# Splitting float64 weights by shifts of the high word, with the low word's share on GpSimd

## Chip, cores and metric

One NeuronCore of a Trainium2 chip runs the whole program in one launch. The metric is the device time of one execution in microseconds, lower is better. Engines are called TensorE (PE, and PEld for its weight loads), VectorE (DVE), ScalarE (ACT), GpSimd (POOL) and SyncE (SP, which issues most of the transfers).

## The reference

Three parts follow each other: an mLSTM attention over 4 x 8 heads of 768 tokens, a mixture of 8 experts with one expert for each token, and a gated MLP over all 3072 tokens of width 320:

```python
def _moe_ref(x, expert_emb, tau, w1, w2):        # N, D, E, F = 3072, 320, 8, 1024
    ...
    for e in range(E):
        mask = expert_idx == e
        h = np.maximum(x[mask] @ w1[e], 0.0)
        out[mask] = gate_w[mask, None] * (h @ w2[e])

def _moe2_ref(x, w_in, w_out):                   # d_ff = 2048
    h = x @ w_in
    g = h * (1.0 / (1.0 + np.exp(-1.702 * h)))
    return (g @ w_out).astype(np.float32)
```

`w_in` (320 x 2048) and `w_out` (2048 x 320) reach the kernel as float64, all other inputs as float32.

## The kernel before

The kernel multiplies in float32 by two parts: a value is split into a high part of type float32r and the rest, and a product is the sum of high times high, high times rest and rest times high. Each weight is therefore split once before it is used.

The expert stage has 64 steps, s = e * 8 + m: expert e (the first four with 512 tokens, the last four with 384) and block m of 128 hidden columns. A step issues, in this order: `h_mm` (8 matmuls into `hp`), `relu_split` (ScalarE writes the high part `hh`, VectorE the rest `hl`, L1094), `tail` of the step before (`o_mm`, three matmuls for each 128 tokens, which need `hh` and `hl`), `split_w` of the expert weights of six steps later (ScalarE casts at L105 and L118, GpSimd subtracts 256 columns at L110, VectorE 64x128 at L111 and 128x320 at L121), `prep_x` in some steps (TensorE transposes the next expert's tokens, ScalarE writes `xh`, VectorE `xl`, L1056), every second step one indirect transfer `meta_put` on GpSimd's queue, and from s = 6 on `convert`.

`convert` prepares the MLP's weights while the expert stage runs. There are 16 blocks m: 384 columns of w_in and 320 of w_out, float64, loaded as pairs of 32-bit words into tile `c` (two buffers). `cvt` turns a pair into a float32 value `fr`: ScalarE scales the low word (L1156), VectorE takes exponent, sign and mantissa out of the high word with four `TENSOR_SCALAR` operations (`ex`, `sb`, `mt`) and joins them with three two-input operations (L1163, L1165, L1167). It is a generator in five parts, of which a call of `convert(n)` runs n: 4 or 3 a step for the experts with 512 tokens and 2 for those with 384, and 3 in each of the 16 steps of block E, the MLP's first. After the last part, `then` splits `fr` one call later like any weight: `split_w1` into `win` (ScalarE cast, GpSimd subtraction L110, VectorE L111), `split_w2` into `wout` (ScalarE L118, VectorE L121). `fr` has two buffers, `ex`, `sb` and `mt` one.

After the expert stage the MLP runs over blocks of tokens, E first: `h_mm` from `win`, `swish_split` (ScalarE sigmoid, VectorE product, ScalarE cast, VectorE `hhl`, L1104 to L1107), `o_mm` from `wout`. `scale_y` multiplies the next block's tokens on GpSimd (L1244).

The whole is issued in a manual schedule: each engine works through its instructions in the order in which the program issues them.

Of the kernel before, what the change touches and what calls it, by code (L numbers as in the profile page):

```python
# [1 line left out]

# [7 lines left out]
F32 = mybir.dt.float32  # L10
F32R = mybir.dt.float32r
BF16 = mybir.dt.bfloat16
I32 = mybir.dt.int32
AF = mybir.ActivationFunctionType
ALU = mybir.AluOpType
# [4 lines left out]
P = 128  # L20
CAP = 512
# [5 lines left out]
def kernel(ctx, tc, qT_in, kT_in, kvo_in, i_gate, f_gate, expert_emb, tau, w12, wio, out, dbg=None):  # L27
# [71 lines left out]
    def split_w1(t, r1):  # L99

        split_w1hi(t, r1)
        split_w1lo(t, r1)
# [10 lines left out]
    def split_w2(t, r2):  # L113
        split_w2hi(t, r2)
        split_w2lo(t, r2, nc.vector)
# [890 lines left out]
    with ExitStack() as mctx:  # L1006
# [137 lines left out]
                tc.add_to_no_dep_group("out", sc.ins)  # L1144


        U32 = mybir.dt.uint32

        def cvt(src, n, then):

            lo, hi = src[:, :, 0], src[:, :, 1]
            ex = mp2.tile([P, n], I32, tag="ex", name="ex", bufs=1)
            sb = mp2.tile([P, n], I32, tag="sb", name="sb", bufs=1)
            mt = mp2.tile([P, n], I32, tag="mt", name="mt", bufs=1)
            fr = mp2.tile([P, n], F32, tag="fr", name="fr")
            nc.scalar.activation(out=fr, in_=lo.bitcast(U32), func=AF.Copy, scale=2.0 ** -52)  # L1156
            nc.vector.tensor_scalar(out=ex, in0=hi, scalar1=20, scalar2=0x7ff, op0=ALU.logical_shift_right, op1=ALU.bitwise_and)  # L1157
            nc.vector.tensor_scalar(out=sb, in0=hi, scalar1=-2147483648, scalar2=None, op0=ALU.bitwise_and)  # L1158
            yield
            nc.vector.tensor_scalar(out=mt, in0=hi, scalar1=0xfffff, scalar2=None, op0=ALU.bitwise_and)  # L1160
            nc.vector.tensor_scalar(out=ex, in0=ex, scalar1=896.0, scalar2=0.0, op0=ALU.subtract, op1=ALU.max)
            yield
            nc.vector.scalar_tensor_tensor(out=fr, in0=mt, scalar=2.0 ** -20, in1=fr, op0=ALU.mult, op1=ALU.add)  # L1163
            yield
            nc.vector.scalar_tensor_tensor(out=ex, in0=ex, scalar=float(2 ** 23), in1=sb, op0=ALU.mult, op1=ALU.add)  # L1165
            yield
            nc.vector.scalar_tensor_tensor(out=fr, in0=fr, scalar=1.0, in1=ex.bitcast(F32), op0=ALU.add, op1=ALU.mult)  # L1167
            late.append(lambda: then(fr))
            yield

        craw, late = {}, []

# [5 lines left out]
        def cvt_all():  # L1178
            for m in range(M2):
                if 0 < m < M2 - 1:  # L1180
                    load_c(m + 1)
                t = craw.pop(m)
                yield from cvt(t[:, 0:3 * P], 3 * P, lambda r, m=m: split_w1(win[:, m], r.rearrange("p (c f) -> p c f", c=3)))
                yield from cvt(t[:, 3 * P:], DM, lambda r, m=m: split_w2(wout[:, m], r))

        tokd = mp1.tile([P, NTILE], I32, name="tokd")
        gated = mp1.tile([P, NTILE], F32, name="gated")
# [189 lines left out]
        with tc.manual_schedule():  # L1377
            load_x0(1)
            flag = nc.values_load(vals_i[0:1, 2 * E:2 * E + 1], min_val=0, max_val=1)
            with tc.If(flag > 0):  # L1380
                general()
            touch()
            load_x0(0)
            for p in range(1, E):
                ids[p] = nc.values_load(vals_i[0:1, p:p + 1], engines=sp, min_val=0, max_val=E - 1)
                if p == 1:
                    load_w(WA // 2 + 1)
                    for c in range(3):
                        prep_x0(1, c)
                    load_x(1)  # L1390
                    load_w(WA // 2 + 2)
            offs = {p: nc.values_load(vals_i[0:1, E + p:E + p + 1], engines=sp, min_val=0, max_val=NT) for p in range(1, E)}

            steps = [(e, m, e * M1 + m) for e in range(E) for m in range(M1)]
            prev = None
            conv = cvt_all()

            def convert(n):

                now, late[:] = late[:], []  # L1400
                for f in now:
                    f()
                for _ in range(n):
                    next(conv, None)

            def tail(p):
                e, m, s = p
                o_mm(e, ("a", s), wslot.pop(s)[1], m == 0, m == M1 - 1)
                if m == M1 - 1:
                    put(e)  # L1410

            for e, m, s in steps:
                h_mm(e, ("a", s), wslot[s][0], EARLY if s in he else 0)
                relu_split(("a", s))
                if s in he:
                    hs_t["a", s] = halves(*he.pop(s)) + hs_t["a", s]
                if prev:
                    tail(prev)
                prev = (e, m, s)
                if 1 <= s < 4:  # L1420
                    prep_x0(0, s - 1)
                if s == 1:
                    gts = gates_1()
                if s == 2:
                    gates_2(*gts)
                if s == 3:
                    order_rows()
                if s == 4:
                    meta_tile()

                for w in [] if s == 0 else [s + WA - 1] if s < WA else [s + WA - 1, s + WA] if s == WA else [s + WA]:
                    if w < NS1:
                        split_w(w)
                        if w % 2 and w // 2 + 3 < NS1 // 2:
                            load_w(w // 2 + 3)
                if e + 1 < E and 2 <= m - (e == 0) < 5:
                    prep_x(e + 1, m - 2 - (e == 0))
                if m == 5 + (e == 0) and e + 2 < E:
                    load_x(e + 2)
                if s % 2 == 0 and 0 <= s // 2 - 3 < NTILE:  # L1440
                    meta_put(s // 2 - 3)
                if s == 7 + 2 * NTILE:
                    meta_get()
                if s == 9 + 2 * NTILE:
                    meta_split()
                if e == E - 1:

                    if m == 1:
                        load_y(E)
                    if m == 3:  # L1450
                        scale_y(E, nc.vector)
                    if 4 <= m < 7:
                        prep_x(E, m - 4)
                    if m == 7:
                        load_y(E + 1)
                if s in (3, 5):
                    load_c((s - 3) // 2)
                if s >= WA:
                    convert(2 if CAPS[e] < CAP else 3 if 2 <= m < 6 else 4)

            def tail2(p):
                blk, m = p
                o_mm(blk, ("b", blk, m), wout[:, m], m == 0, m == M2 - 1)
                if m == M2 - 1:
                    put_out(blk)

            left = [prev]
            for blk in range(E, len(COLS)):
                for m in range(M2):
                    h_mm(blk, ("b", blk, m), win[:, m])  # L1470
                    swish_split(("b", blk, m))
                    left.append((blk, m))
                    while len(left) > (1 if ncol(blk) == CAP else 2):
                        p = left.pop(0)
                        (tail2 if len(p) == 2 else tail)(p)
                    if blk == E:
                        convert(3)
                    nxt = blk + 1
                    if nxt < len(COLS):
                        t = m - (2 if blk == E else 0)  # L1480
                        small = ncol(blk) < CAP
                        if t == 2:
                            scale_y(nxt, nc.vector if small else nc.gpsimd)
                        for j in range(ncol(nxt) // GH):
                            t0 = t - 3 * j
                            if 3 <= t0 < 5:
                                planes(nxt, j, t0 - 3)
                            w0 = t0 - (8 if small else 6)
                            if 0 <= w0 < 2:
                                words(nxt, j, w0)  # L1490
                            if 2 <= w0 < 5:
                                parts(nxt, j, w0 - 2)
                        if t == 8 and nxt + 1 < len(COLS):
                            load_y(nxt + 1)
            for p in left:
                tail2(p)
            if dbg is not None:
                nc.sync.dma_start(out=dbg["slot"], in_=slot_i)
                nc.sync.dma_start(out=dbg["lg"], in_=logit_all.rearrange("p t e -> p (t e)"))
                nc.sync.dma_start(out=dbg["ss"], in_=ss_all)  # L1500
# [62 lines left out]
```

## Time and profile before

| | us |
|---|---|
| median of 3 runs | 809.84 |
| lowest and highest of them | 806.26, 811.72 |
| profiled execution, its time | 813.04 |
| profiled execution, span of the trace | 811.3 |

In the profile a group of instructions is named by engine, line, operation and the tiles that it writes and reads (`out<-in`, shapes as partitions x elements). Its time is given as busy time and as the mean of one instruction; an idle time behind it is what the engine waited for just before, and what ended that. The timeline gives for each instruction its start, its duration, and in brackets the wait before it. TensorE's clock is given as a share of 2.4 GHz; its lower level is 1.2 GHz.

### The profile page before, as it was taken

Reading aid. Unit: us, or ns where it says so; the run is one execution under the profiler, and the core shown is the slowest. Engines: PE = TensorE matmul, PEld = TensorE weight load, DVE = VectorE, ACT = ScalarE, POOL = GpSimd, SP = SyncE. Lnnn points to the kernel's source line nnn. Section 1 sums busy time; section 2 is a strip of 40 time slices with the busy share of each in tenths; the row PEclk is TensorE's granted clock in tenths of the full one; section 3 lists DMA queues with packets and bytes.
Section 4 is the critical chain, followed back from the end, with each engine's and each line's share of the span. In section 5 each row is a group of like instructions: output and inputs, shape, how many; then the busy total and the mean of one; then the engine's idle time right before and its main releaser. Section 6 shows DMA issues by size and latency. Waiting matters only on the chain.

```text
span 811.3 us, 13142 instructions
## 1 busy us (share of the span) xinstructions
PE 749.3 (92%) x4708; PEld 695.9 (86%) x4708; DVE 577.4 (71%) x1209; ACT 340.8 (42%) x802; POOL 246.8 (30%) x362
## 2 busy tenths in 40 slices
PE   6789888998798999989998899999999999999995
PEld 6789888888797787888888789899899898999995
DVE  7887979988499999999997645555554554445542
ACT  4343332434464455555554334333343334334442
POOL 4553456686134334444531100300300300201011
PEclk9798978989899999999999999999999999999998
DMA  6977757662465645567743212021120110200100
GB/s 194 313 260 215 270 191 248 209 236 85 154 224 161 219 148 198 179 182 216 206 111 99 64 21 59 33 41 37 43 69 1 53 40 1 71 1 20 35 17 16
DMA packets 70302, 100.19 MB, mean 123 GB/s; under 512 B 31120, under 2 KB 56472, under 8 KB 70232
## 3 DMA queue, kind: packets, MB, share of 16 engines
q1 hardware_dynamic: 67160, 91.41, 37.0%
q0 software_dynamic: 3072, 7.89, 2.8%
q8 instruction: 38, 0.62, 0.3%
q14 instruction: 32, 0.26, 0.1%
HBM read 77.53 MB, written 17.82 MB: 118 GB/s over the span
## 4 chain that ended last, share of the span: by engine, by line
issue 41%; DVE 17%; PE 6%; POOL 5%; ACT 1%; POOLq 0%; DVEq 0%; ACTq 0%
DVE w L121 3%; POOL out_dram L1140 3%; DVE hl L1094 3%; PE hp L138 3%; DVE w L111 2%; DVE fr L1167 2%; POOL xr L1244 2%; DVE ex L1165 1%; PE acc L1119 1%; DVE fr L1163 1%; DVE ex L1157 1%; DVE mt L1160 1%; DVE xl L1056 1%; DVE sb L1158 1%; PE acc L1118 1%
## 5 line engine op out<-in xcount | busy, mean ns | idle before, releaser
L1105 DVE TENSOR_TENSOR sg<-hp,sg 128x512 f32<-128x512 f32 (+1 forms) x112 | 68.8, 615 | 100.7 <-ACT sg L1104 100.6
L138 PE MATMUL hp<-xh,win 128*128 128x512 f32 (+1 forms) x560 | 130.7, 363 | 0.0
L1107 DVE TENSOR_TENSOR hhl<-sg,hhl 128x512 fp32r<-128x512 f32 (+1 forms) x112 | 71.6, 639 | 70.0 <-ACT hhl L1106 70.0
L1117 PE MATMUL acc<-wout,hhl 128*128 128x320 f32 x384 | 118.4, 308 | 2.4 <-ACT hhl L1106 2.4
L1119 PE MATMUL acc<-wout,hhl 128*128 128x320 f32 x384 | 118.9, 310 | 0.2 <-DVE hhl L1107 0.2
L1118 PE MATMUL acc<-wout,hhl 128*128 128x320 f32 x384 | 118.7, 309 | 0.0
L1140 POOL DMA_INDIRECT out_dram<-o,tokd x24 | 23.7, 989 | 312.0 <-ACT o L1127 308.4
L1104 ACT ACTIVATE sg<-hp 128x512 f32<-128x512 f32 (+1 forms) x112 | 60.4, 539 | 133.0 <-PE hp L138 132.8
L138 PEld LDWEIGHTS hp<-xh,win 128*128 128x128 f32 x560 | 94.6, 189 | 10.5
L1106 ACT CAST hhl<-sg 128x512 fp32r<-128x512 f32 (+1 forms) x112 | 62.6, 559 | 81.2 <-DVE sg L1105 81.2
L138 PE MATMUL hp<-xl,win 128*128 128x512 f32 (+1 forms) x336 | 86.1, 365 | 0.0
L110 POOL TENSOR_TENSOR w<-r,w 128x256 fp32r<-128x256 f32 x58 | 48.2, 832 | 122.1 <-ACT w L105 119.7
L1119 PE MATMUL acc<-w,hl 128*128 128x320 f32 x212 | 68.9, 325 | 15.8 <-DVE hl L1094 15.4
L1117 PEld LDWEIGHTS acc<-wout,hhl 128*128 128x128 f32 x384 | 72.1, 188 | 6.2 <-ACT hhl L1106 2.8
L138 PE MATMUL hp<-xh,w 128*128 128x384 f32 (+2 forms) x320 | 75.9, 368 | 0.0
L1118 PEld LDWEIGHTS acc<-wout,hhl 128*128 128x128 f32 x384 | 72.2, 188 | 3.4
L1119 PEld LDWEIGHTS acc<-wout,hhl 128*128 128x128 f32 x384 | 72.2, 188 | 0.5 <-DVE hhl L1107 0.4
L138 PEld LDWEIGHTS hp<-xl,win 128*128 128x128 f32 x336 | 59.3, 190 | 11.2 <-DVE xl L1284 0.2
L1117 PE MATMUL acc<-w,hh 128*128 128x320 f32 x212 | 65.5, 309 | 0.0
L1118 PE MATMUL acc<-w,hh 128*128 128x320 f32 x212 | 65.4, 309 | 0.0
L360 DVE TENSOR_TENSOR_SCAN pm<-fb,ident_h 128x1024 f32<-128x1024 f32 x23 | 56.3, 2447 | 6.9 <-DMA fb<-dec 5.5
L400 PE MATMUL sp<-qT,kblk 120*128 120x128 f32 x384 | 57.8, 313 | 3.4 <-DVE wm L405 3.4
(315 smaller groups left out, 1526.4 us busy)
## 6 DMA issues: line engine op xcount, KB each, us to landing
r<-in_w_dram SPq DMA_DIRECT2D x32, 704.0 KB
fb<-dec SPq DMA_DIRECT2D x23, 512.0 KB
kvo<-in_kvo_dram SPq DMA_DIRECT2D x24, 480.0 KB
c<-in_wio_dram SPq DMA_DIRECT2D x16, 704.0 KB
rows<-zt SPq DMA_DIRECT2D x8, 640.0 KB
qT<-in_qT_dram SPq DMA_DIRECT2D x24, 180.0 KB
xr<-y SPq DMA_DIRECT2D x5, 640.0 KB
kblk<-in_kT_dram SPq DMA_DIRECT2D x48, 60.0 KB
```

The lines of the kernel that those rows point to most:

```text
L110: eng.tensor_tensor(out=t[:, 3 * P:5 * P].rearrange("p (c f) -> p c f", c=2), in0=r1[:, 0:2], in1=hif[:, 0:2], op=ALU.subtract)
L138: nc.tensor.matmul(hp, a, b, start=(i == 0), stop=(i == len(seq) - 1))
L360: nc.vector.tensor_tensor_scan(out=pm[u].rearrange("p h t -> p (h t)"), data0=fb[u].rearrange("p h t -> p (h t)"), data1=ident_h.rearrange ...
L400: nc.tensor.matmul(sp[:, h - hs.start], kblk[u % NLD][0:KR, h // 3, h % 3, :], qT[u][0:KR, h // 3, :], start=True, stop=True)
L1104: nc.scalar.activation(out=sg, in_=hp, func=AF.Sigmoid, scale=1.702)
L1105: nc.vector.tensor_tensor(out=g, in0=hp, in1=sg, op=ALU.mult)
L1106: nc.scalar.copy(hh, g)
L1107: nc.vector.tensor_tensor(out=hl, in0=g, in1=hh.bitcast(F32), op=ALU.subtract)
L1117: nc.tensor.matmul(a, hh, w[:, 0:DM], start=first, stop=False)
L1118: nc.tensor.matmul(a, hh, w[:, DM:2 * DM], start=False, stop=False)
L1119: nc.tensor.matmul(a, hl, w[:, 0:DM], start=False, stop=last)
L1140: sc = nc.gpsimd.indirect_dma_start(out=out, out_offset=bass.IndirectOffsetOnAxis(ap=tokd[:, ti:ti + 1], axis=0), in_=o[:, i], in_offset=None)
```

## The change

`cvt` is rewritten. The value's upper 32 bits come from the high word w1 by shifts and masks. ScalarE takes w1's absolute value as a float32 pattern (Abs), GpSimd limits it by a max and a min (`LEAST`, `MOST`), VectorE shifts it left by 3 with a mask and joins the sign bits (`shifts`), and takes from the result the power of two `pw`. In the next call (`rests`) ScalarE writes the high part `hi` straight into `win` or `wout`, GpSimd multiplies the scaled low word by `pw`, and GpSimd subtracts `hi` from the value. In the call after that (`sums`) VectorE adds the two rests into `lo`; for w_in with a second operation on 64 partitions.

So a matrix takes a start and three further calls of `convert`. A call first runs what is due of earlier matrices, then adds `thirds` to a counter and starts one matrix for each full three: 2 thirds a step for experts with 512 tokens, 1 for those with 384, 1 in each step of block E. `fr` and the new tile `rest` have two buffers, `pw` one. `split_w1` and `split_w2` are no longer called for these weights.

```diff
-        def cvt(src, n, then):
-            lo, hi = src[:, :, 0], src[:, :, 1]
...
-            nc.scalar.activation(out=fr, in_=lo.bitcast(U32), func=AF.Copy, scale=2.0 ** -52)
-            nc.vector.tensor_scalar(out=ex, in0=hi, scalar1=20, scalar2=0x7ff, op0=ALU.logical_shift_right, op1=ALU.bitwise_and)
-            nc.vector.tensor_scalar(out=sb, in0=hi, scalar1=-2147483648, scalar2=None, op0=ALU.bitwise_and)
-            yield
-            nc.vector.tensor_scalar(out=mt, in0=hi, scalar1=0xfffff, scalar2=None, op0=ALU.bitwise_and)
-            nc.vector.tensor_scalar(out=ex, in0=ex, scalar1=896.0, scalar2=0.0, op0=ALU.subtract, op1=ALU.max)
-            yield
-            nc.vector.scalar_tensor_tensor(out=fr, in0=mt, scalar=2.0 ** -20, in1=fr, op0=ALU.mult, op1=ALU.add)
-            yield
-            nc.vector.scalar_tensor_tensor(out=ex, in0=ex, scalar=float(2 ** 23), in1=sb, op0=ALU.mult, op1=ALU.add)
-            yield
-            nc.vector.scalar_tensor_tensor(out=fr, in0=fr, scalar=1.0, in1=ex.bitcast(F32), op0=ALU.add, op1=ALU.mult)
-            late.append(lambda: then(fr))
-            yield
+        LEAST, MOST = (struct.unpack("<f", struct.pack("<I", w))[0] for w in (0x38100000, 0x47EFFFFF))
+        def cvt(src, n, hi, lo):
+            w0, w1 = src[:, :, 0], src[:, :, 1]
+            pw = mp2.tile([P, n], I32, tag="pw", name="pw", bufs=1)
+            fr = mp2.tile([P, n], I32, tag="fr", name="fr")
+            rest = mp2.tile([P, n], F32, tag="rest", name="rest")
+            top, nl = fr.bitcast(F32), lo.shape[-1]
+            nc.scalar.activation(out=rest, in_=w0.bitcast(U32), func=AF.Copy, scale=2.0 ** -52)
+            nc.scalar.activation(out=top, in_=w1.bitcast(F32), func=AF.Abs)
+            nc.gpsimd.tensor_scalar(out=top, in0=top, scalar1=LEAST, scalar2=MOST, op0=ALU.max, op1=ALU.min)
+            def shifts():
+                nc.vector.tensor_scalar(out=fr, in0=fr, scalar1=3, scalar2=0x3ffffff8, op0=ALU.logical_shift_left, op1=ALU.bitwise_and)
+                nc.vector.scalar_tensor_tensor(out=fr, in0=w1, scalar=-0x40000000, in1=fr, op0=ALU.bitwise_and, op1=ALU.bitwise_or)
+                nc.vector.tensor_scalar(out=pw, in0=fr, scalar1=-0x800000, scalar2=None, op0=ALU.bitwise_and)
+            def rests():
+                nc.scalar.copy(hi, top)
+                nc.gpsimd.tensor_tensor(out=rest, in0=rest, in1=pw.bitcast(F32), op=ALU.mult)
+                nc.gpsimd.tensor_tensor(out=top, in0=top, in1=hi.bitcast(F32), op=ALU.subtract)
+            def sums():
+                nc.vector.tensor_tensor(out=lo, in0=top[:, 0:nl], in1=rest[:, 0:nl], op=ALU.add)
+                if nl < n:
+                    nc.vector.tensor_tensor(out=hi[64:P, nl:n], in0=top[64:P, nl:n], in1=rest[64:P, nl:n], op=ALU.add)
+            late.extend([(1, shifts), (2, rests), (3, sums)])
...
-                yield from cvt(t[:, 0:3 * P], 3 * P, lambda r, m=m: split_w1(win[:, m], r.rearrange("p (c f) -> p c f", c=3)))
-                yield from cvt(t[:, 3 * P:], DM, lambda r, m=m: split_w2(wout[:, m], r))
+                cvt(t[:, 0:3 * P], 3 * P, win[:, m, 0:3 * P], win[:, m, 3 * P:5 * P])
+                yield
+                cvt(t[:, 3 * P:], DM, wout[:, m, 0:DM], wout[:, m, DM:2 * DM])
+                yield
...
-            def convert(n):
-                now, late[:] = late[:], []
+            due = [0]
+            def convert(thirds):
+                now, late[:] = [f for k, f in late if k == 1], [(k - 1, f) for k, f in late if k > 1]
                 for f in now:
                     f()
-                for _ in range(n):
+                due[0] += thirds
+                while due[0] >= 3:
+                    due[0] -= 3
                     next(conv, None)
...
-                    convert(2 if CAPS[e] < CAP else 3 if 2 <= m < 6 else 4)
+                    convert(1 if CAPS[e] < CAP else 2)
...
-                        convert(3)
+                        convert(1)
```

## Rows read from the trace of the kernel before

**Rows 1.** The page, busy time of each engine over the span, with its share and its instructions.

```profile
PE 749.3 (92%) x4708; PEld 695.9 (86%) x4708; DVE 577.4 (71%) x1209; ACT 340.8 (42%) x802; POOL 246.8 (30%) x362
```

**Rows 2.** Busy time by stretch: the stretch in us from the span's start, its length, the busy time and instructions of PE, PEld, DVE, ACT and POOL, then the granted clock, the share of the DMA engines and GB/s. The stretches are the experts with 512 tokens from step 8 on, those with 384 up to step 63, and the beginning of block E.

```profile
240.56:347.20 106.64, 97.29 (x526) 84.74 (x525) 103.81 (x225) 53.89 (x122) 41.53 (x57) 0.98 0.56 178
347.20:447.18 99.98, 91.88 (x560) 87.53 (x559) 93.72 (x206) 54.27 (x130) 37.28 (x54) 1.00 0.60 165
447.18:470.00 22.82, 20.27 (x103) 17.59 (x102) 13.95 (x23) 8.95 (x16) 3.50 (x2) 0.93 0.17 55
```

**Rows 3.** Waits from 240.56 to 347.2 us: who waited for whom, us in total, times, the longest.

```profile
PE acc L1119 <- DVE hl L1094: 9.2, 12, 1.9
...
ACT fr L1156 <- DVE win L111: 7.4, 3, 3.7
...
ACT fr L1156 <- DVE wout L121: 5.0, 2, 2.6
```

**Rows 4.** Groups by line from 240.56 to 447.18 us, VectorE's and then GpSimd's tensor operations: count, busy us, mean ns of one, idle time before them.

```profile
L121 DVE TENSOR_TENSOR w<-r,w 128x320 fp32r<-128x320 f32 x51 | 30.4, 595 | 1.5
L111 DVE TENSOR_TENSOR w<-r,w 64x128 fp32r<-64x128 f32 x51 | 20.1, 395 | 1.6
L1167 DVE SCALAR_TENSOR_TENSOR fr<-fr,ex 128x384 f32<-128x384 f32 (+1 forms) x30 | 17.6, 586 | 0.7
...
L1157 DVE TENSOR_SCALAR ex<-c 128x320 int32<-128x320 int32 (+1 forms) x30 | 14.5, 483 | 0.7
L1158 DVE TENSOR_SCALAR sb<-c 128x320 int32<-128x320 int32 (+1 forms) x30 | 13.4, 447 | 0.0
...
L1161 DVE TENSOR_SCALAR ex<-ex 128x320 int32<-128x320 int32 (+1 forms) x30 | 12.5, 415 | 0.0
...
L110 POOL TENSOR_TENSOR w<-r,w 128x256 fp32r<-128x256 f32 x50 | 41.8, 835 | 98.7 <-ACT w L105 96.4 <-PE acc L1119 2.2
...
L110 POOL TENSOR_TENSOR win<-fr,win 128x256 fp32r<-128x256 f32 x15 | 11.8, 787 | 14.7 <-ACT win L105 14.7
```

**Rows 5.** Timeline of ScalarE: the relus (L1093) of steps 8, 15, 16, 17, 32 and 63, and the conversion's low word (L1156) between those of 15 and 16. Start us, duration us, and in brackets the wait before it.

```profile
240.56 0.60 ACT L1093 ACTIVATE hh<-hp 128x512 fp32r<-128x512 f32 x1 [1.86 <-PE hp L138]
...
271.60 0.60 ACT L1093 ACTIVATE hh<-hp 128x512 fp32r<-128x512 f32 x1 [0.85 <-PE hp L138]
...
277.61 0.51 ACT L1156 ACTIVATE fr<-c 128x320 f32<-128x320 uint32 x1 [2.59 <-DVE wout L121]
278.02 0.58 ACT L1093 ACTIVATE hh<-hp 128x512 fp32r<-128x512 f32 x1
...
280.31 0.61 ACT L1093 ACTIVATE hh<-hp 128x512 fp32r<-128x512 f32 x1
...
347.20 0.47 ACT L1093 ACTIVATE hh<-hp 128x384 fp32r<-128x384 f32 x1
...
447.18 0.49 ACT L1093 ACTIVATE hh<-hp 128x384 fp32r<-128x384 f32 x1 [0.82 <-PE hp L138]
```

**Rows 6.** Timeline of GpSimd and VectorE, two places where they work at once.

```profile
300.98 0.91 POOL L110 TENSOR_TENSOR w<-r,w 128x256 fp32r<-128x256 f32 x1 [1.73 <-ACT w L105]
...
301.20 0.90 DVE L1160 TENSOR_SCALAR mt<-c 128x384 int32<-128x384 int32 x1
...
334.21 0.85 POOL L110 TENSOR_TENSOR w<-r,w 128x256 fp32r<-128x256 f32 x1 [1.79 <-ACT w L105]
...
334.38 0.55 DVE L1056 TENSOR_TENSOR xl<-xt,xh 128x384 fp32r<-128x384 f32 x1
```

**Rows 7.** Timeline of VectorE where GpSimd does nothing on tensors.

```profile
303.47 0.29 DVE L111 TENSOR_TENSOR w<-r,w 64x128 fp32r<-64x128 f32 x1
303.79 0.49 DVE L121 TENSOR_TENSOR w<-r,w 128x320 fp32r<-128x320 f32 x1
304.20 0.55 DVE L1165 SCALAR_TENSOR_TENSOR ex<-ex,sb 128x384 int32<-128x384 int32 x1
...
312.52 0.35 DVE L1157 TENSOR_SCALAR ex<-c 128x384 int32<-128x384 int32 x1
312.79 0.35 DVE L1158 TENSOR_SCALAR sb<-c 128x384 int32<-128x384 int32 x1
...
314.07 0.55 DVE L1165 SCALAR_TENSOR_TENSOR ex<-ex,sb 128x384 int32<-128x384 int32 x1
314.54 0.68 DVE L1094 SCALAR_TENSOR_TENSOR hl<-hp,hh 128x512 fp32r<-128x512 f32 x1
```

**Rows 8.** Groups of GpSimd by line over the whole span, shapes kept apart.

```profile
L497 POOL TENSOR_TENSOR sg<-sg,dn 128x320 f32<-128x320 f32 x22 | 16.1, 734 | 27.2 <-DVE dn L490 15.0 <-DVE logit_all L541 4.0 <-ACT vp_in L381 3.5
...
L1244 POOL TENSOR_TENSOR xr<-xr,gated 128x1536 f32<-128x1536 f32 x4 | 11.1, 2767 | 0.0
...
L199 POOL TENSOR_SCALAR_AFFINE_SELECT tri<-tri 128x128 f32<-128x128 f32 x1 | 0.3, 286 | 0.0
```

**Rows 9.** The beginning of block E: timeline of VectorE and TensorE, and the busy time from 460 to 470 us (columns as in rows 2).

```profile
454.37 2.78 DVE L1160 TENSOR_SCALAR mt<-c 128x320 int32<-128x320 int32 x1
...
459.49 0.42 PE L1117 MATMUL acc<-wout,hhl 128*128 128x320 f32 x1 [2.39 <-ACT hhl L1106]
...
460.00:470.00 10.00, 9.84 (x48) 8.77 (x48) 4.01 (x8) 2.80 (x5) 0.00 (x0) 0.83 0.00 0
```

**Rows 10.** Timeline of ScalarE, a load of a function table ahead of the first sigmoid.

```profile
448.07 1.28 ACT L1104 ACT_TABLE_LOAD   x1
```

More of the change, by code (lines that the diff above doesn't have):

```diff
@@ L1 @@
+import struct
 from contextlib import ExitStack
@@ L1147 @@
         U32 = mybir.dt.uint32
-        def cvt(src, n, then):
-            lo, hi = src[:, :, 0], src[:, :, 1]
[L1152 to L1155, printed above, removed]
-            nc.scalar.activation(out=fr, in_=lo.bitcast(U32), func=AF.Copy, scale=2.0 ** -52)
-            nc.vector.tensor_scalar(out=ex, in0=hi, scalar1=20, scalar2=0x7ff, op0=ALU.logical_shift_right, op1=ALU.bitwise_and)
-            nc.vector.tensor_scalar(out=sb, in0=hi, scalar1=-2147483648, scalar2=None, op0=ALU.bitwise_and)
-            yield
-            nc.vector.tensor_scalar(out=mt, in0=hi, scalar1=0xfffff, scalar2=None, op0=ALU.bitwise_and)
-            nc.vector.tensor_scalar(out=ex, in0=ex, scalar1=896.0, scalar2=0.0, op0=ALU.subtract, op1=ALU.max)
-            yield
-            nc.vector.scalar_tensor_tensor(out=fr, in0=mt, scalar=2.0 ** -20, in1=fr, op0=ALU.mult, op1=ALU.add)
-            yield
-            nc.vector.scalar_tensor_tensor(out=ex, in0=ex, scalar=float(2 ** 23), in1=sb, op0=ALU.mult, op1=ALU.add)
-            yield
-            nc.vector.scalar_tensor_tensor(out=fr, in0=fr, scalar=1.0, in1=ex.bitcast(F32), op0=ALU.add, op1=ALU.mult)
-            late.append(lambda: then(fr))
-            yield
```

## Prediction

> **What bounds the kernel now.** I read the page's busy shares first, then the busy time by stage, then the waits and the single instructions of the stage that the change touches. Over the whole span TensorE is the busiest engine at 92% [rows 1], but the change acts in the expert stage (steps s = 6 to 63) and in the first 16 steps of the block after it, so that stage has to be read by itself. It has two halves, cut at the starts of the relu of steps 8, 32 and 63 [rows 5]: 24 steps with 512 tokens (4.44 us each) and 31 steps with mostly 384 (3.22 us each). In the first half VectorE is busy for 103.8 of 106.6 us and TensorE for 97.3; in the second it is 93.7 and 91.9 of 100.0 [rows 2]. So VectorE sets the pace in the first half and nearly so in the second, and TensorE waits for its `hl` (9.2 us in the first half [rows 3]). TensorE's idle time is 9.3 and 8.1 us, and 2.6 us from there to 470 us [rows 2]: about 20 us is the most that a lighter VectorE can give back there, whatever is taken off it.
>
> The second thing to see is that VectorE and GpSimd stand in each other's way. A `TENSOR_SCALAR` of 384 columns takes 0.35 us; the one that started at 301.20, while GpSimd's subtraction of 300.98 ran, took 0.90 and ended just after it. The `xl` subtraction at 334.38, which reads PSUM, took 0.55 beside a GpSimd subtraction [rows 6], as long as an undisturbed two-input operation of that size [rows 7]. So GpSimd's tensor operations hold up those of VectorE that read SBUF alone, and not those with a PSUM operand. How much in all: six groups of VectorE, count times (mean less the clean duration): `w` at L121 51 x (595 - 485), `w` at L111 51 x (395 - 290), L1157 30 x (483 - 340), L1158 30 x (447 - 335), L1161 30 x (415 - 330), L1167 30 x (586 - 520): 23.3 us [rows 4], the clean ones being undisturbed durations of like forms [rows 7], a mean over 384 and 320 columns where a group holds both. GpSimd's tensor time there is 41.8 + 11.8 = 53.6 us [rows 4]. With the smaller groups left out, each microsecond of it costs VectorE about half of one.
>
> **The change part by part.** All costs are per pair of float64 blocks m (384 columns of w_in, 320 of w_out); there are 16.
>
> VectorE's share. Undisturbed operations follow each other every 0.27 us (`TENSOR_SCALAR`, 384), 0.47 (two inputs, 384) and 0.41 (two inputs, 320) [rows 7]; for a 320 `TENSOR_SCALAR` I take 0.25, an estimate from the first of them. Before: w_in 4 x 0.27 + 3 x 0.47 + 0.29 for the 64-partition subtraction = 2.78; w_out 4 x 0.25 + 3 x 0.41 + 0.41 = 2.64. Sum 5.4 us. After: w_in 2 x 0.27 + 0.47 + about 0.34 (256-column sum, between 0.29 and 0.41) + 0.29 = 1.64; w_out 2 x 0.25 + 0.41 + 0.41 = 1.32. Sum 3.0. A bitwise two-input operation has no row; I price it as the arithmetic ones, bounded by 0.27 and twice 0.47.
>
> GpSimd's share. Before, one 256-column subtraction of 0.79 us [rows 4]. After, two two-input operations and one max/min for each matrix. A 320-column operation took 0.73 us and one of 1536 columns 2.77 [rows 8], so 1.67 ns a column, and 384 columns cost 0.84. The one-input max/min has no row: above 0.29 (a 128x128 select [rows 8]), below 0.84; I take 0.55 and 0.50. Sum 2 x 0.84 + 0.55 + 2 x 0.73 + 0.50 = 4.2 us, so 3.4 us more per m.
>
> How many m fall in each half. Before, a step takes 4, 3 or 2 of 10 parts of an m: steps 8 to 31 hold 84 parts, 8.4 m, and 32 to 62 hold 62, 6.2 m. After, `convert(2)` adds two thirds of a matrix and `convert(1)` one: 16 matrices, 8.0 m, and 5.2 m. About two m move into block E, where VectorE has room (13.9 of 22.8 us busy at its start [rows 2]); with that cover they cost nothing, and were it gone 2 x 3.0 us.
>
> First half: VectorE 8.0 x 3.0 - 8.4 x 5.4 = -21.4 us; GpSimd 8.0 x 4.2 - 8.4 x 0.79 = +27.0 us, half of it felt by VectorE, +13.5. Net -7.9. Second half: 5.2 x 3.0 - 6.2 x 5.4 = -17.9; GpSimd 5.2 x 4.2 - 6.2 x 0.79 = +16.9, felt +8.5; net -9.4, but only 8.1 us of TensorE's time is idle and not all of it VectorE's: I take -6.5.
>
> The new wait. `fr` and `rest` have two buffers, and a matrix now lives three calls of `convert`. In the first half matrices start in two of three steps, so each start needs the buffers whose last readers, the sums on VectorE, are issued in that very call. ScalarE runs in order: its copy of the low word waits until VectorE has done this step's `hl`, both `w` subtractions and the sums; behind it stand Abs and the next step's relu, for which `hl` and then TensorE wait. Before, the same wait is there but seldom: 7.4 + 5.0 us at L1156, five times [rows 3]. What one costs: the relu of 271.60 was followed only 6.42 us later, after a wait of 2.59, and the next one 2.29 us after that [rows 5]. Lower bound: nothing, because the two steps together took 8.71, 4.36 each, and TensorE had work in hand. Upper bound: the eight starts of w_in, behind two sums and GpSimd's two operations, each lose 6.42 - 4.44 = 2.0 us for good, 16 us. I take a little under the middle, +7, since the pair of steps shows the lower end. In the second half a matrix starts every third step, its buffer is free three steps earlier, and the wait is not there.
>
> ScalarE gets one Abs more per matrix, about 0.5 us like L1156 (0.51 [rows 5]); it is busy for about half of the time in both halves [rows 2], so this costs nothing but what the wait above contains. The loads of `c` are held one step longer by the shifts, against three steps of slack: nothing.
>
> Block E. Before, GpSimd's `xr` scaling ran at once with a VectorE operation of the conversion (2.78 us, where a clean one of 384 columns takes 0.35), TensorE stood for 2.39 us, and the mean granted clock was 0.83 between 460 and 470 us [rows 9], that is, after the idle stretch it was partly at 1.2 GHz, the lower of its two levels. After, that scaling stands behind w_in of m = 14 in GpSimd's queue, at m = 4, where VectorE has less waiting. Gain 0 to 2.6 + 1.7 us; new GpSimd operations may each hold `hhl` up: I take -1.
>
> Sum: -7.9 + 7 - 6.5 - 1 = -8.4, say -8 us. The profiled execution took 813.04 us for a span of 811.3, 3.2 above the median of the runs; 813.0 - 8 = 805.0, and for the median 809.84 - 8 = **802 us**.
>
> One rule of the Trainium skill bears on the felt half (SBUF — State Buffer, section "Who interferes with whom"): of a GpSimd operation and a VectorE operation that wants the shared ports, the one that starts second is blocked until the first ends. The single rows [rows 6] agree. Taken for every microsecond of GpSimd it would make the felt part 27 and 17 us, the whole and not half, and the sum +14 us, 824; it speaks against the change, and is the far end of rival B.
>
> **The rivals.**
>
> A. The buffer wait costs nothing, because TensorE runs ahead and the short step follows the long one, as after 278.02 [rows 5]. Then -7.9 - 6.5 - 1 = -15: 795 us. For it: the two steps of 4.36. Against: before, five such waits fell among 24 steps; now there are 16.
>
> B. Slower: GpSimd takes the port nearly the whole time. Its queue is then the chain: sums wait for its operations, and VectorE's felt share rises from a half. Each tenth more costs 4.4 us; at 0.68 the gain is gone, and at 0.9 the sum is -8 + 0.4 x 43.9 = +10: 820 us. For it: GpSimd's operations come in pairs, three to a matrix, and VectorE, freed of arithmetic, has mostly SBUF operations left. Against: VectorE, too, holds GpSimd up and idles more, so that they can alternate.
>
> C. Abs makes ScalarE load another table. Each load is 1.28 us [rows 10]; two for each of 32 matrices would be 82 us, 892 us. Against: relu, copies and casts share the stage, and the load that ends it stands ahead of the first sigmoid [rows 10]. The Trainium skill says the same (ScalarE: Activation LUTs, section "Table sets: the hidden batching unit"): abs lies in every set. No run here shows an Abs.
>
> D. The change doesn't ease the stage: VectorE's freed time is filled by waiting for GpSimd in program order, step for step, and TensorE's pace stays: 810 us.
>
> **How the numbers follow.** Forecast (wait half paid, 797 to 808): 0.45. A: 0.25. B: 0.18. C: 0.02. D: 0.10. Something over 1% (8 us) is what a measurement of this kernel tells from no change. Faster by over 1% is A and 0.18 of the forecast's cases, 0.43; within 1% is its other 0.27, D and 0.03 of B, 0.40; slower is 0.15 of B and C, 0.17. The range reaches into A almost to its bound of 20 us (790) and into B short of its price, leaving out C and most of B: 791 to 818 us.
>
> **What would show it.** Right: VectorE's busy time falls in both halves, by less than its instructions do; GpSimd's rises to over half of the first half; ScalarE shows a wait for the sums at its low-word copy in most starts of the first half and none in the second; the 31 steps of the second half come in 93 to 95 us; the first half stays within a few microseconds of 106.6. Wrong: a first half under 100 us (the wait is hidden, A), or over 114 with VectorE's means far above the clean ones (B); a table load in the stage (C); TensorE idle in block E beside GpSimd's new operations.

## The result: slower, 1.0138 times the kernel before

| | median us | ratio to the kernel before, 95% interval |
|---|---|---|
| changed kernel, 4 runs | 820.94 | 1.0138 (1.0094 to 1.0181) |
| the same, measured again | 817.21 | 1.0106 (1.0057 to 1.0155) |

802 us (791 to 818) was forecast; 820.94 lies above the range, on the other side of no change. The second row was measured on another chip; its profiled execution shows the same picture, with 216.6 us from step 8 to step 63 against 218.3, so a difference of 2 us in such a stretch says nothing.

The stage is cut as before, at the relus of steps 8, 32 and 63; behind them the beginning of block E. Lines of the changed file stand one or a few lower than before (L122 was L121, L1095 was L1094). Busy time by stretch of the changed kernel, columns as in [rows 2]:

```profile
240.07:360.51 120.44, 103.21 (x533) 88.15 (x531) 103.22 (x158) 58.70 (x135) 85.92 (x96) 0.96 0.47 152
360.51:458.40 97.89, 89.12 (x551) 86.43 (x552) 89.11 (x152) 56.78 (x136) 70.53 (x81) 1.00 0.55 167
458.40:481.20 22.80, 22.80 (x129) 20.60 (x128) 12.03 (x23) 12.27 (x23) 9.53 (x8) 1.00 0.26 87
```

The first half takes 120.4 us instead of 106.6, the second 97.9 instead of 100.0, and from step 63 to the end 360.8 instead of 364.1 (span less the relu of step 63). So the loss sits in the first half. VectorE runs 158 instructions there instead of 225 and is still busy for 103.2 us, only 0.6 less than before; its idle time grew from 2.8 to 17.2 us. GpSimd more than doubled, 41.5 to 85.9.

Groups by line from 240.07 to 458.40 us of the changed kernel, VectorE's, then GpSimd's (as [rows 4]):

```profile
L122 DVE TENSOR_TENSOR w<-r,w 128x320 fp32r<-128x320 f32 x50 | 43.5, 869 | 1.5
...
L112 DVE TENSOR_TENSOR w<-r,w 64x128 fp32r<-64x128 f32 x50 | 28.6, 573 | 1.9 <-ACT w L106 0.3
L1167 DVE SCALAR_TENSOR_TENSOR fr<-c,fr 128x384 int32<-128x384 int32 (+1 forms) x27 | 22.1, 819 | 0.9
L1166 DVE TENSOR_SCALAR fr<-fr 128x384 int32<-128x384 int32 (+1 forms) x27 | 22.1, 819 | 0.0
L1168 DVE TENSOR_SCALAR pw<-fr 128x384 int32<-128x384 int32 (+1 forms) x27 | 13.0, 483 | 1.5
...
L111 POOL TENSOR_TENSOR w<-r,w 128x256 fp32r<-128x256 f32 x50 | 40.7, 816 | 12.4 <-ACT w L106 12.3
L1163 POOL TENSOR_SCALAR fr<-fr 128x384 f32<-128x384 f32 (+1 forms) x27 | 39.4, 1458 | 33.1 <-ACT fr L1162 33.1
L1172 POOL TENSOR_TENSOR rest<-rest,pw 128x384 f32<-128x384 f32 (+1 forms) x27 | 26.7, 989 | 12.4 <-DVE pw L1168 12.3
...
L1173 POOL TENSOR_TENSOR fr<-fr,win 128x384 f32<-128x384 f32 x14 | 14.7, 1047 | 0.6 <-ACT win L1171 0.6
L1173 POOL TENSOR_TENSOR fr<-fr,wout 128x320 f32<-128x320 f32 x13 | 12.4, 954 | 0.0
```

The busy time of `hl`, which reads PSUM, is as before; a line of the kernel before, then one of the changed kernel, same stretches:

```profile
L1094 DVE SCALAR_TENSOR_TENSOR hl<-hp,hh 128x384 fp32r<-128x384 f32 (+1 forms) x55 | 33.3, 606 | 0.0
L1095 DVE SCALAR_TENSOR_TENSOR hl<-hp,hh 128x384 fp32r<-128x384 f32 (+1 forms) x55 | 33.5, 609 | 16.0 <-ACT hh L1094 15.8
```

Nobody touched L122 and L112, the expert weights' own subtractions, and they went from 595 and 395 ns to 869 and 573. With the clean durations of the prediction the stalls are 50 x (869 - 485) + 50 x (573 - 290) + 27 x (819 - 520) + 27 x (819 - 340) + 27 x (483 - 340) = 58 us, against 23 before. The max/min (L1163) takes 1.46 us, not 0.55.

Six of VectorE's operations in this stretch take 2.67 to 3.45 us; the longest of the conversion and the expert weights in the same stretch before took 1.64. Each of the six starts while GpSimd issues the transfer `meta` (L1235) and ends only when the product and the difference behind it (L1172, L1173) are both done; in the longest it is the expert subtraction behind these two as well:

```profile
382.54 3.45 DVE L112 TENSOR_TENSOR w<-r,w 64x128 fp32r<-64x128 f32 x1
383.14 1.03 POOL L1172 TENSOR_TENSOR rest<-rest,pw 128x384 f32<-128x384 f32 x1
384.12 1.03 POOL L1173 TENSOR_TENSOR fr<-fr,win 128x384 f32<-128x384 f32 x1
385.11 0.73 POOL L111 TENSOR_TENSOR w<-r,w 128x256 fp32r<-128x256 f32 x1
```

So in these places VectorE wasn't let in between GpSimd's operations. The six make about 15 of the 58 us.

Waits of the first half of the changed kernel (as [rows 3]):

```profile
ACT rest L1161 <- DVE win L1179: 28.5, 8, 4.3
...
DVE hl L1095 <- ACT hh L1094: 14.1, 15, 1.8
PE acc L1120 <- DVE hl L1095: 13.2, 13, 2.7
ACT rest L1161 <- DVE wout L1176: 11.3, 6, 1.9
```

The wait of ScalarE's low-word copy came in 14 of 16 starts, 39.8 us, where it had been 12.4 in 5. One long step, relu of step 16 to relu of step 17, timeline of the three engines:

```profile
276.60 0.60 ACT L1094 ACTIVATE hh<-hp 128x512 fp32r<-128x512 f32 x1
...
284.63 0.54 ACT L1161 ACTIVATE rest<-c 128x384 f32<-128x384 uint32 x1 [4.29 <-DVE win L1179]
285.08 0.53 ACT L1162 ACTIVATE fr<-c 128x384 f32<-128x384 f32 x1
285.51 0.58 ACT L1094 ACTIVATE hh<-hp 128x512 fp32r<-128x512 f32 x1
...
277.48 1.14 DVE L1166 TENSOR_SCALAR fr<-fr 128x320 int32<-128x320 int32 x1
278.65 1.19 DVE L1167 SCALAR_TENSOR_TENSOR fr<-c,fr 128x320 int32<-128x320 int32 x1
...
282.84 1.07 DVE L122 TENSOR_TENSOR w<-r,w 128x320 fp32r<-128x320 f32 x1
283.83 0.41 DVE L1176 TENSOR_TENSOR win<-fr,rest 128x256 fp32r<-128x256 f32 x1
284.26 0.29 DVE L1179 TENSOR_TENSOR win<-fr,rest 64x128 fp32r<-64x128 f32 x1
286.12 0.69 DVE L1095 SCALAR_TENSOR_TENSOR hl<-hp,hh 128x512 fp32r<-128x512 f32 x1 [1.57 <-ACT hh L1094]
286.84 0.29 DVE L112 TENSOR_TENSOR w<-r,w 64x128 fp32r<-64x128 f32 x1
...
277.17 1.26 POOL L1172 TENSOR_TENSOR rest<-rest,pw 128x384 f32<-128x384 f32 x1
278.39 1.10 POOL L1173 TENSOR_TENSOR fr<-fr,win 128x384 f32<-128x384 f32 x1
...
282.58 0.97 POOL L1173 TENSOR_TENSOR fr<-fr,wout 128x320 f32<-128x320 f32 x1
285.70 1.50 POOL L1163 TENSOR_SCALAR fr<-fr 128x384 f32<-128x384 f32 x1 [2.14 <-ACT fr L1162]
```

From top to bottom: relu to relu is 8.91 us. VectorE's shifts (277.48, 278.65) last until GpSimd's product and difference let go, 1.14 and 1.19 us instead of 0.3 to 0.5; L122 at 282.84 the same. Then the sums end at 284.55, and only now ScalarE's copy, Abs and the next relu go, while VectorE stands for 1.57 us. Two prices lie in one chain: VectorE is held up by GpSimd's operations ("the port" from here on), and ScalarE waits for VectorE. At 286.84 VectorE's L112 keeps its 0.29 us although GpSimd's max/min runs; of all 50 such operations 11 met a max/min and no two-input operation, and all took 0.29.

### The profile page after: what moved, and what is told of

It is laid out like the page before. It is cut to its first block, busy times and chain, and to the rows that moved or that the text cites. A ratio compares the mean times of both kernels' runs of the same rounds, so it can differ in the third digit from the quotient of the medians.

```text
span 819.2 us, 13174 instructions
## 1 busy us (share of the span) xinstructions
PE 751.6 (92%) x4708; PEld 697.1 (85%) x4708; DVE 577.1 (70%) x1097; ACT 352.8 (43%) x834; POOL 344.5 (42%) x442
## 4 chain that ended last, share of the span: by engine, by line
issue 36%; DVE 16%; PE 13%; POOL 4%; ACT 4%; POOLq 0%; DVEq 0%; ACTq 0%
PE hp L139 6%; DVE w L122 3%; POOL out_dram L1141 3%; PE acc L1120 2%; DVE w L112 2%; DVE fr L1166 2%; DVE fr L1167 2%; PE acc L1119 2%; PE acc L1118 2%; DVE hl L1095 2%; POOL xr L1258 1%; DVE xl L1057 1%; ACT fr L1162 1%; ACT hh L1094 1%; ACT w L106 1%
## 5 line engine op out<-in xcount | busy, mean ns | idle before, releaser
L1105 ACT ACTIVATE sg<-hp 128x512 f32<-128x512 f32 (+1 forms) x112 | 60.4, 539 | 123.6 <-PE hp L139 123.6
L139 PEld LDWEIGHTS hp<-xh,win 128*128 128x128 f32 x560 | 93.9, 188 | 10.3
L139 PE MATMUL hp<-xh,w 128*128 128x384 f32 (+2 forms) x320 | 77.7, 374 | 0.0
L1118 PE MATMUL acc<-w,hh 128*128 128x320 f32 x212 | 66.8, 315 | 4.7 <-ACT hh L1094 3.9
L1119 PE MATMUL acc<-w,hh 128*128 128x320 f32 x212 | 66.1, 312 | 0.0
L1163 POOL TENSOR_SCALAR fr<-fr 128x384 f32<-128x384 f32 (+1 forms) x32 | 46.7, 1460 | 41.9 <-ACT fr L1162 41.9
L1120 PEld LDWEIGHTS acc<-w,hl 128*128 128x128 f32 x212 | 40.5, 191 | 26.5 <-DVE hl L1095 26.0
```

What stands on the lines that cost most here:

```text
L139: nc.tensor.matmul(hp, a, b, start=(i == 0), stop=(i == len(seq) - 1))
L1105: nc.scalar.activation(out=sg, in_=hp, func=AF.Sigmoid, scale=1.702)
L1118: nc.tensor.matmul(a, hh, w[:, 0:DM], start=first, stop=False)
L1119: nc.tensor.matmul(a, hh, w[:, DM:2 * DM], start=False, stop=False)
L1120: nc.tensor.matmul(a, hl, w[:, 0:DM], start=False, stop=last)
L1163: nc.gpsimd.tensor_scalar(out=top, in0=top, scalar1=LEAST, scalar2=MOST, op0=ALU.max, op1=ALU.min)
```

## The experiments

Three theories. W: ScalarE's wait for the sums in the starting call is the cause. P: GpSimd's two-input operations hold VectorE up. M: the slow max/min fills GpSimd's queue. Each kernel is the changed one with the edit shown. The ratio is to the kernel before on the same chip. The step before the relu of step 32 is long in some versions and the one behind it short (8.9 and 1.8 us with the change), and in others not (4.5 and 4.4 with late starts and the rests on VectorE), so the two halves are best read as a sum ("stage": 206.6 us before, 218.3 with the change).

| kernel | ratio, 95% interval | first half, second half | stage |
|---|---|---|---|
| late start | 1.0119 (1.0085 to 1.0153) | 109.3, 102.1 | 211.4 |
| max/min on VectorE | 1.0122 (1.0082 to 1.0162) | 116.8, 98.2 | 215.1 |
| rests on VectorE | 0.9895 (0.9856 to 0.9934) | 106.8, 93.9 | 200.6 |
| late start, rests on VectorE | 0.9934 (0.9901 to 0.9967) | 95.6, 98.3 | 193.9 |
| late start for 512 tokens alone | 1.0003 (0.9966 to 1.0040) | 108.8, 101.9 | 210.7 |
| the same, rests on VectorE | 0.9852 (0.9788 to 0.9916) | 95.6, 96.7 | 192.3 |
| rests on VectorE, idle two-input operations | 1.0014 (0.9979 to 1.0050) | 112.1, 95.9 | 208.0 |
| rests on VectorE, idle one-input operations | 0.9919 (0.9886 to 0.9953) | 105.7, 94.9 | 200.7 |
| late for 512, rests and max/min on VectorE | 0.9806 (0.9757 to 0.9855) | 97.0, 98.4 | 195.5 |
| late for 512, product on GpSimd, difference on VectorE | 0.9926 (0.9882 to 0.9969) | 103.1, 98.7 | 201.8 |

**Late start.**

```diff
-            due = [0]
+            due, starts = [0], [0]
...
                 while due[0] >= 3:
                     due[0] -= 3
-                    next(conv, None)
+                    starts[0] += 1
+            def start():
+                while starts[0]:
+                    starts[0] -= 1
+                    next(conv, None)
...
                 relu_split(("a", s))
+                start()
...
                     swish_split(("b", blk, m))
+                    if blk == E:
+                        start()
```

> The changed kernel, but a matrix is started (low word and Abs on ScalarE, max/min on GpSimd) right behind the next step's relu instead of at the end of convert; shifts, rests and sums stay where they are. Theory W (ScalarE's low-word copy waits for the sums of the same call, and holds the next relu up; 39.8 us of such waits in 14 starts of the first half): the first half falls from 120.4 us to 102 to 108 and the whole from 821 to 802 to 808. Theory P (GpSimd's two-input operations stall VectorE, about 60 us in the expert stage, and the wait for the sums is only where VectorE's lateness shows): less than 5 us come back, 816 to 820. Theory M (the max/min of 1.46 us fills GpSimd's queue): no gain, 819 to 823.

The first half came in at 109.3 us, just above what W expected, and the stage gave back 6.9 us. But the stretch from step 63 to the end rose from 360.8 to 366.8, and the whole, 816.20 us, is no measurable step from the change. In block E shifts now follow their start in the same step, and VectorE waits for the max/min. Two waits of this kernel, in block E's beginning and then in the first half:

```profile
DVE fr L1166 <- POOL fr L1163: 7.5, 5, 1.8
DVE hl L1095 <- ACT hh L1094: 1.8, 1, 1.8
```

The second is VectorE's wait for the relu, 14.1 us in 15 with the change. So W is a part of the loss in the stage and not all.

**Max/min on VectorE.**

```diff
-            nc.gpsimd.tensor_scalar(out=top, in0=top, scalar1=LEAST, scalar2=MOST, op0=ALU.max, op1=ALU.min)
             def shifts():
+                nc.vector.tensor_scalar(out=top, in0=top, scalar1=LEAST, scalar2=MOST, op0=ALU.max, op1=ALU.min)
```

> The changed kernel with the max/min moved from GpSimd to VectorE, at the head of shifts. Theory M: GpSimd loses 28 x 1.46 = 41 us in the expert stage, VectorE gains 28 x 0.27 = 8 us; if GpSimd's queue is the chain the whole falls to 806 to 812. Theory W: VectorE's chain in each long step grows by 0.27 us or more, 820 to 825. Theory P: the max/min is a one-input operation and VectorE's operations beside it were not stretched, so no gain, 818 to 824.

816.35 us, its ratio within the interval of the change; the stage is 3.2 us shorter. GpSimd loses the most expensive of its new operations and no gain like the 806 to 812 that M named comes of it, so M falls as the main cause. The max/min isn't shown to be free: VectorE took over some 8 us of work with it, and no time was lost by that.

**Rests on VectorE.**

```diff
-                nc.gpsimd.tensor_tensor(out=rest, in0=rest, in1=pw.bitcast(F32), op=ALU.mult)
-                nc.gpsimd.tensor_tensor(out=top, in0=top, in1=hi.bitcast(F32), op=ALU.subtract)
+                nc.vector.tensor_tensor(out=rest, in0=rest, in1=pw.bitcast(F32), op=ALU.mult)
+                nc.vector.tensor_tensor(out=top, in0=top, in1=hi.bitcast(F32), op=ALU.subtract)
```

> The changed kernel with the multiplication of the low word and the subtraction of the high part on VectorE instead of GpSimd; the max/min stays on GpSimd. VectorE gets 2 x 0.47 + 2 x 0.41 = 1.76 us per block m more, 13.2 us over the expert stage's 13.2 m ... 23 us; GpSimd loses 54 us of two-input operations. Theory P: at 0.63 us of VectorE stall for each, 34 us of stalls go, net -11: 808 to 814. Theory W: the chain before each start gets longer by the two operations and shorter by the stalls; 815 to 826.

799.02 us, a larger gain than P expected. Busy time by stretch of this kernel:

```profile
235.58:342.35 106.77, 98.12 (x530) 83.84 (x529) 97.55 (x190) 58.80 (x136) 55.35 (x64) 1.00 0.56 173
342.35:436.20 93.85, 89.16 (x556) 86.77 (x555) 85.10 (x173) 56.62 (x135) 51.69 (x59) 1.00 0.63 175
```

VectorE runs 190 instructions in the first half instead of 158 and is busy for 97.6 us instead of 103.2: more work in less time. Over the stage its busy time is 182.7 us against 192.3, and its idle time 18.0 against 26.0. None of its operations on weights takes longer than 1.6 us here, and L122 is back at 671 ns:

```profile
L122 DVE TENSOR_TENSOR w<-r,w 128x320 fp32r<-128x320 f32 x50 | 33.5, 671 | 1.5
```

**Both.** The edits of the late start and of the rests together.

> Both: starts behind the next relu and the two-input operations on VectorE. W and P both a part of the cause: the sum of the two gains, 792 to 800, below the kernel before. W alone: as the late start alone or some microseconds above it, 803 to 812. P alone: as the rests on VectorE alone, 808 to 814.

The stage is the sum of the two, 193.9, but block E takes its price again (371.1 us from step 63 to the end). So the whole is 803 us, outside the 792 to 800 that stood for both causes, and it is the stage that speaks for them.

**Late start where it pays.** The late start, but `convert(1)`, that is 384 tokens and block E, starts at once:

```diff
                     starts[0] += 1
+                if thirds == 1:
+                    start()
...
                     swish_split(("b", blk, m))
-                    if blk == E:
-                        start()
```

> The changed kernel with the starts behind the next relu for the experts with 512 tokens alone; with 384 tokens and in block E they stay at the end of convert. If the late start costs something only where shifts follow it in the same step with VectorE otherwise free (VectorE waited 7.5 us for the max/min in block E, the second half was 102.1 against 97.9 us), this keeps its gain and not its price: first half about 109, second 98, from there to the end 361, 803 to 808 in all. If the late start merely shifts the lateness into the next half, 812 to 818.

> Starts behind the next relu for the experts with 512 tokens alone, and the two-input operations on VectorE. If port and wait are two prices that add up: first half 95.6 (as with both everywhere), second 93.9 and the rest 361 (as with the rests on VectorE alone), 786 to 792. If they are one price counted twice: 796 to 800, as with the rests on VectorE alone.

Without and with the rests on VectorE: 808.09 and 794.31 us, the first even with the kernel before, the second faster than it. The price in block E is gone (360.9 and 361.2). The second halves, 101.9 and 96.7 us, missed the 98 and 93.9 expected, mostly by where the cut falls: from step 34 to step 63 they are 92.4 and 88.1 against 91.2 with the change and 87.2 with the rests on VectorE. 794.31 lies between the two expectations for the second kernel. With the changed kernel and the rests on VectorE these make a square: in the stage the wait is worth 218.3 - 210.7 = 7.6 us with the rests on GpSimd and 200.6 - 192.3 = 8.3 with them on VectorE; the rests are worth 17.7 and 18.4. In the stage the two prices add up. The whole times give the wait 9 to 13 us (from 817.21 or 820.94 to 808.09) and 4.7 (799.02 to 794.31); their intervals are too wide to tell whether these differ. In the last kernel TensorE is busy as long as VectorE (busy time of its first half):

```profile
234.68:330.24 95.56, 91.70 (x515) 81.79 (x513) 91.80 (x184) 60.00 (x136) 57.18 (x64) 1.00 0.62 192
```

**The port by itself.** Into the kernel with the rests on VectorE, at each start, three operations of GpSimd on a constant whose result nobody reads, with two inputs or (same tile `idle`) with one:

```diff
+        idle = mp1.tile([P, P], F32, name="idle")
...
+            for _ in range(3):
+                nc.gpsimd.tensor_tensor(out=idle, in0=ident, in1=ident, op=ALU.add)
```

```diff
+            for _ in range(3):
+                nc.gpsimd.tensor_scalar(out=idle, in0=ident, scalar1=LEAST, scalar2=MOST, op0=ALU.max, op1=ALU.min)
```

> The kernel with the rests on VectorE (799 us), and at each start three 128x128 two-input additions on GpSimd, of a constant onto a tile that nobody reads; nothing waits for them but GpSimd's own queue. By the price of 1.67 ns a column they take about 0.4 us each, 27 x 1.2 = 33 us in the expert stage. Theory P (two-input operations of GpSimd hold up VectorE's operations on SBUF): 0.4 to 0.6 us of VectorE stall for each us, 13 to 20 us, of which the first half feels most: 805 to 815. Theories W and M: GpSimd has room for them (55 of 107 us busy in the first half), 798 to 801.

> The same with three one-input max/min operations of 128x128 in place of the additions. Theory P, by the rows in which VectorE's operations beside a max/min kept their clean durations: no stall, 798 to 802, although GpSimd works longer on them (0.5 to 1.0 us each). If any work of GpSimd on SBUF holds VectorE up: as much or more than with the two-input ones, 805 to 820.

Groups of GpSimd by line from 235 to 436 us, first the kernel with two-input operations:

```profile
L1168 POOL TENSOR_TENSOR idle<-ident 128x128 f32<-128x128 f32 x78 | 36.0, 462 | 4.1
```

and the one with one-input operations:

```profile
L1168 POOL TENSOR_SCALAR idle<-ident 128x128 f32<-128x128 f32 x80 | 57.7, 721 | 4.5
```

Over the whole stage these are 37.2 and 58.3 us. Busy time by stretch, first with two-input and then with one-input operations:

```profile
234.49:346.56 112.07, 100.68 (x530) 86.64 (x529) 104.08 (x190) 58.98 (x135) 79.64 (x112) 0.97 0.51 164
346.56:442.47 95.91, 91.06 (x556) 88.43 (x555) 87.19 (x173) 56.83 (x136) 64.90 (x92) 0.98 0.63 171
...
234.01:339.74 105.73, 99.36 (x533) 84.14 (x531) 96.98 (x190) 58.82 (x136) 89.42 (x112) 1.00 0.57 175
339.74:434.68 94.94, 88.49 (x551) 86.44 (x552) 87.18 (x175) 56.71 (x135) 73.85 (x92) 1.00 0.67 174
```

The two-input ones made the stage 208.0 us, the one-input ones left it at 200.7 (200.6 without either). In whole times, 808.81 against 800.70 on the same chip. VectorE, with the same work, is busy for 191.3 us with the first and 184.2 with the second (182.7 without either). GpSimd's queue can't be the reason: the one-input operations fill it longer. So work of GpSimd that no one waits for costs time if it has two inputs, and hardly any if it has one, and P is shown. Its price here is smaller than the 13 to 20 us expected: 7.4 us of stage, 0.20 for each microsecond of GpSimd.

**Two finer steps.** To the 794 us version, the max/min on VectorE too (edit above), or the product alone back on GpSimd.

> The version with late starts for 512 tokens and the rests on VectorE (794 us), with the max/min on VectorE too, so that GpSimd does nothing for these weights. The max/min adds 0.27 us to VectorE for each matrix, 28 x 0.27 = 8 us in the expert stage, and takes 1.46 us out of the way between Abs and shifts. If VectorE, still 96% busy in the first half, is the bound there: 795 to 801. If waits for the max/min are: 785 to 792.

> The same version (794 us) with the multiplication of the low word back on GpSimd and the subtraction on VectorE. VectorE saves 0.47 + 0.41 us per block m, 13.2 m, 11.6 us; GpSimd's product takes 27 x 0.99 = 27 us and at 0.4 to 0.6 us of stall for each costs 11 to 16 us. Theory P: the two cancel or the move loses a little, 793 to 800. If one GpSimd operation at a time hides behind VectorE's operations on PSUM: 784 to 791.

> The changed kernel itself once more, on the chip of these two runs, so that they can be compared: 816 to 822, ratio 1.009 to 1.018.

With all of it on VectorE 794.89 us, no measurable step from 794.31, and between the two expectations. With the product on GpSimd 801.23, just above what P expected: VectorE is spared 11.6 us of work, and yet the kernel takes 6.9 us more (6.3 against the 794.89 of the same chip) and the stage 9.5. That kernel's product on GpSimd (group by line over the stage), then its busy time by stretch:

```profile
L1172 POOL TENSOR_TENSOR rest<-rest,pw 128x384 f32<-128x384 f32 (+1 forms) x27 | 26.9, 996 | 11.6 <-DVE pw L1168 11.5
...
234.25:337.30 103.05, 93.93 (x515) 83.16 (x513) 95.78 (x169) 59.16 (x136) 72.62 (x79) 0.98 0.55 177
337.30:436.03 98.73, 93.03 (x569) 90.73 (x570) 90.00 (x170) 57.49 (x137) 60.66 (x71) 0.98 0.59 167
```

So a microsecond of that product costs the kernel (11.6 + 6.9) / 27 = 0.69 to (11.6 + 9.5) / 27 = 0.78 us. The changed kernel itself came out at 817.21, as expected.

Not all of such a price is VectorE held up; a part is waiting that goes with it. What VectorE's own busy time shows can be set apart, with the work that moved (1.76 x 13.2 = 23 us and 11.6 us, both estimates of the expectations) added back:

| two-input work of GpSimd | GpSimd, us | in VectorE's busy time, us | for each us | in the stage, us | for each us |
|---|---|---|---|---|---|
| both rests, in the changed kernel | 53.8 | 192.3 - 182.7 + 23 = 33 | 0.61 | 17.7 + 23 = 41 | 0.76 |
| the product alone | 26.9 | 185.8 - 180.5 + 11.6 = 17 | 0.63 | 9.5 + 11.6 = 21 | 0.78 |
| idle additions | 37.2 | 191.3 - 182.7 = 9 | 0.23 | 7.4 | 0.20 |

Why the idle ones cost less for each microsecond wasn't tested. They are short, and beside them no operation of VectorE was held through several: the longest in that stage, the `xr` scaling apart, took 1.46 us.

## Why the prediction was wrong

- **What is held up, and the saved work: right.** Operations with a PSUM operand aren't held up (`hl` has a mean of 606 ns before and 609 after). VectorE's busy time less its stalls fell from 197.5 - 23 = 174 to 192.3 - 58 = 134 us, by 40; the prediction took 21.4 + 17.9 = 39.3 off.
- **The step that failed: "half of it felt by VectorE".** The mechanism was right and the term mis-sized. 13.5 and 8.5 us, 22 in all, were taken as felt; the stalls grew by 58 - 23 = 35 us, 0.80 of the 43.9 us that the prediction gave GpSimd and past the 0.68 at which rival B put the end of the gain. So VectorE's busy time in the two halves fell by 5.2 us, not by 17.3 (7.9 and 9.4). That it is the rests which do it is shown by moving them to VectorE: 23 us more work for it, and a stage 17.7 us shorter. The prediction took the share of before, when 53.6 us of GpSimd's operations came singly. Now they come in pairs, as B said, and the six operations held through such a pair alone make 15 us.
- **The wait: right in kind, and in the stage in size.** +7 was taken, 7.6 and 8.3 us are what its removal gives back. It appeared where it should, in 14 of 16 starts of the first half, and not among the waits of the second. VectorE's idle time in the stage rose by 16.9 us, though, against 9.9 in the prediction (7, and 2.9 of the second half's gain that could not be used). The other 7 go with the rests on GpSimd: without them the idle time is 18.0 us instead of 26.0. These 7 and the 12 us of busy time are the whole miss of the stage, which was to get 7.4 us shorter and got 11.7 longer.
- **The signs.** The first half, 120.4 us, is past the 114 that the prediction named as B's sign. The second half took 97.9 us, not 93 to 95.
- **GpSimd's operations took longer than priced:** the max/min 1.46 us, not 0.55, above the upper bound of 0.84; product and difference 0.88 to 1.09 by form, not 0.73 and 0.84. The last two rows of VectorE in [rows 7] aren't undisturbed either: GpSimd's L110 ran from 313.66 for 1.55 us beside them. VectorE's durations there are the clean ones all the same; GpSimd's 1.55 us stand against a mean of 0.84 [rows 4], and that VectorE holds GpSimd up had no term in the sum. The max/min's length isn't the cause (theory M): one-input operations hardly hold VectorE up.
- **Block E: -3.3 us instead of -1**, from step 63 to the end. TensorE isn't idle from 458 to 481 us, and the granted clock is 1.00 there, 2.4 GHz, where [rows 9] had 0.83 after the 2.39 us stand. That the later scaling on GpSimd is the reason was argued, not tested.
- **Rivals.** A (no wait) and D (no change) fell. C fell: the load ahead of the first sigmoid (459.68 us, L1105) is the only one from step 8 on, as before; Abs brought none, as the Trainium skill says (ScalarE: Activation LUTs, section "Table sets: the hidden batching unit"). B came true in VectorE's felt share, with the wait beside it; that sums wait for GpSimd's operations, its other half, is not among the waits. The rule cited in the prediction (the Trainium skill, SBUF — State Buffer, section "Who interferes with whom") was nearer to the chip than my half: 0.80 measured, where full blocking would be 1.

## What to carry to other kernels

Moving elementwise work from VectorE to GpSimd pays only where VectorE isn't busy on SBUF at that time. The price isn't nothing, and a share that was measured when such operations were rare doesn't carry over: 0.43 us for each microsecond before (23 of 53.6), about 0.6 in VectorE's busy time and three quarters with the waits for the rests here, 0.2 for idle additions. Ask whether long two-input operations of GpSimd will stand behind each other: here VectorE was held through two of them at a time.

A buffer ring must outlast the number of calls that a value lives, or the start has to stand behind the work that the waiting engine owes the critical chain; here the second was tried, and a third buffer was not. The wait could be counted ahead from readers and calls, the port's price could not. Keeping the rests on VectorE and starting late where it pays gave a kernel of 794 us, 1.5% below the one before.

## Not expected of the hardware

GpSimd's one-input max/min, 1.46 us in the mean, took longer than its two-input product (0.99), yet held VectorE up little: 58.3 us of such operations lengthened a stage of 200.6 us by 0.1 and VectorE's busy time by 1.5, while 37.2 us of two-input ones lengthened them by 7.4 and 8.6. They don't leave it wholly alone: some operations of VectorE that met a max/min and no two-input operation were 0.1 to 0.5 us longer than clean.

One operation of VectorE can be held through two GpSimd operations in a row, and once through three: 3.45 us where 0.29 is clean.
